# A planned sort-attention and Fourier-mix kernel: mixed V stored and gathered back with keys on partitions, in place of a mix that produces that layout directly

## Chip, core and metric

One NeuronCore of one Trainium2 chip runs the whole program. The metric is the device time of one execution in microseconds (us); less is better. Before the change three executions took 284.15, 284.58 and 284.76 us, median 284.58. The profiled execution is the one of 284.76 us; its span, from the first to the last instruction, is 283.0 us, so 1.76 us lie outside the span.

Engines: PE (matrix unit, with PEld for its weight loads), DVE (vector), ACT (scalar), POOL (GpSimd) and SP (sync). POOL and SP issue the DMAs.

## What is computed

The inputs are q, k, v of shape (4, 8, 768, 64), a sort_net of (4, 8, 8, 8) and two MLP weights, 512x2048 and 2048x512. Each of 32 (batch, head) pairs has 8 blocks of 96 tokens. The reference, cut to what matters:

```
P = sort_net
for _ in range(5):                       # Sinkhorn: rows, then columns
    P = exp(P - max(P, -1)); P = P / sum(P, -1); P = P / sum(P, -2)
k_sorted = einsum('bhij,bhjcd->bhicd', P, k_b)      # blocks of K mixed
v_sorted = einsum('bhij,bhjcd->bhicd', P, v_b)      # blocks of V mixed
attn = softmax(q_b @ k_sorted.T / 8)                # inside each block
x = attn @ v_sorted                                 # heads side by side
u = x + real(fft(fft(x, axis=tokens), axis=model))
out = u + relu(norm(u) @ w_ch1) @ w_ch2
```

## The kernel before

The four batches are worked one after another through the same stages: attention (attn), the Fourier stage in two parts (dft1, dft2), normalisation, and the MLP in two token halves (mlp(b, 0) and mlp(b, 1)). V is mixed for two batches at once: "pair 0" is batches 0 and 1, "pair 1" batches 2 and 3.

The program is written as a list of operations with costs, priorities and dependences (Plan.add). A planner (Plan.schedule) plays them through on a model of the engines when the program is built and so fixes one order for each engine and each DMA queue; on the chip every engine runs its order strictly one after another and waits by semaphores. "late" and the second number of a cost are the planner's allowances for latency; they change the order only. DMA issues are such operations too: most loads stand in POOL's order, small copies, DMA transposes and most stores in SP's. The planner drives towards a goal, the end of dft2(0, 0), since the MLP work (lines 1281 and 1302), which is most of PE's, can begin only after it. Where PE would idle before that goal, dummy matmuls ("spin", line 1397) are put into its order; their number is fixed when the program is built.

The way of V for a pair t, which the change rewrites:

- load_v (line 520) brings v with the 128 (head, block) rows of a pair on the partitions, into nat[t], as two halves of 48 tokens of each block. v_path then sums V over the 96 tokens of a block on PE with an identity weight (line 693, tag psm, 12 matmuls of 512 columns) and on DVE (line 701, tag vb), for the block means vbn.
- eight copies (pair 0, on DVE and ACT, line 678, "vcx<-hr") or eight subtractions of the mean (pair 1, on DVE, line 726) rearrange nat into vcx, in which the 96 tokens of one feature lie side by side.
- bdv_make makes the block-diagonal mixing matrix bdv16 (line 780) from the Sinkhorn result.
- v_mix (line 732) multiplies 128 columns of vcx, as weights, with bdv16: 64 matmuls of 128x128 (line 742), for pair 0 with 64 more that subtract the mean (line 745). Since vcx is the weight, the result has the tokens (keys) on the partitions. Sixteen copies of 96x512 per pair (line 678, "vsf<-bank") move it from PSUM into vsb, from which av (line 1021) reads it.

Attention of a pair of heads hp: kq matmuls (line 927) and their copies into ks, q transposes (line 957) and copies into qt, scores (line 982), exp on ACT (line 991), subtraction of one into the eb buffers (line 1004 on DVE, 1006 on ACT), av (line 1021), and on DVE the reciprocal and scaling into rt (lines 1033 and 1036). The four eb buffers are two pairs of heads. They are set to zero at the start by POOL (line 537).

From rt, DVE and PE go through dft1 (lines 1053 to 1103), y (ACT, line 1111), dft2 (lines 1181, 1185, 1169), u (lines 1193 and 1205), statistics (1219, 1221), ny (ACT, 1225 and 1228), un (1241 and 1245), transposes (1260) and ut, to the MLP.

Of the kernel before, what the change touches and what calls it, by code (L numbers as in the profile page):

```python
# [18 lines left out]
D = 64  # L19
# [25 lines left out]
GT = 384  # L45


def _consts():
# [56 lines left out]
    vrow = np.zeros((1, 128, D + 1), f16)  # L105
# [9 lines left out]
    def as32(m):  # L115
# [8 lines left out]
                rows=rows, erow=np.tile(erow, (1, 4)), vrow=vrow, pack=pack)  # L124


class Op:
    __slots__ = ("n", "costs", "fn", "preds", "succs", "left", "ready", "prio",
                 "vts", "fresh", "nbytes", "end", "start", "eng", "tag",
                 "crit", "late")  # L130
# [13 lines left out]
class Plan:  # L144
# [14 lines left out]
    def add(self, costs, fn, r=(), w=(), prio=None, nbytes=0, tag="",  # L159
            after=()):  # L160
# [7 lines left out]
        o.preds, o.succs, o.vts, o.fresh = set(after), [], [], []  # L168
        for k in r:
            o.preds.update(self.wr.get(k, ()))  # L170
# [41 lines left out]
    def schedule(self):  # L212
# [48 lines left out]
        while todo:  # L261
# [70 lines left out]
            for s in o.succs:  # L332
                s.left -= 1
                for x in s.costs:
                    s.ready[x] = max(s.ready[x],
                                     o.end + (0.03 if x == e else self.XL))
                if s.left == 0:
                    for x in s.costs:
                        avail[x].append(s)
# [13 lines left out]
def pe(t):  # L353
    return {"PE": (t, t + 0.17)}
# [12 lines left out]
def kernel(  # L367
# [22 lines left out]
    def many(name, n, shape, dtype):  # L390
# [18 lines left out]
    vcx = ct("vcx", [128, 128 * D + 2], F16)  # L409
    dtab = vcx[:, 6144:7168].rearrange("p (c w) -> p c w", c=4)  # L410
    lt = vcx[0:97, 7168:7168 + LTW]
    vsf = ct("vsf", [97, 128 * (D + 1)], F16)
    vsb = vsf[:, 0:128 * (D + 1)].rearrange("p (g w) -> p g w", w=D + 1)
    eb4 = ct("eb4", [97, 4, EW], F16)
    P.pool("eb", [eb4[:, n, :] for n in range(4)])
# [14 lines left out]
    many("un", 2, [128, DM], F16)  # L430
# [9 lines left out]
             vcx[:, 7938:8194].bitcast(F32).rearrange(  # L440
# [15 lines left out]
    phl = [hr[1].rearrange("p a b -> p (a b)")[  # L456
        0:32, 64 * n:64 * n + 64].rearrange("p (i j) -> p i j", i=NB)
        for n in range(2)]
    pk, pvh, pvl = [hr[1].rearrange("p a b -> p (a b)")[
        0:32, 1024 * n:1024 * n + 1024].rearrange("p (i x) -> p i x", i=NB)  # L460
        for n in (2, 4, 5)]
    pws = hr[1].rearrange("p a b -> p (a b)")[0:32, 3072:3232].bitcast(F32)
# [9 lines left out]
    def load(dst, src, nbytes, w, prio, eng="POOL", r=(), after=()):  # L472
# [3 lines left out]
                  prio=prio, nbytes=nbytes, tag="load", after=after)  # L476
        o.late = 6.0 if after else 0.0
# [6 lines left out]

    slot = {}
# [14 lines left out]
    def load_qk(nm, b, hf, prio):  # L500
        after = lns[1:2] if b > 1 else ()
        src = {"k": k, "q": q}[nm]
        if nm == "q" and b in QB:
            for h in range(4):
# [4 lines left out]
                    260000, [("kq", slot[nm, b, hf], h)], prio + 0.01 * h,  # L509
# [4 lines left out]
                 "h (p r) d -> p h (r d)", r=6), 786432,  # L514
# [5 lines left out]
    def load_v(t, hf, prio):  # L520
        load(nat[t].rearrange("p (c d) -> p c d", d=D)[
            :, 48 * hf:48 * hf + 48, :],
            vv[128 * t:128 * t + 128, 48 * hf:48 * hf + 48, :], 1572864,
            [("nat", t, hf)] + (hk(0)[8 * hf:8 * hf + 8] if t == 0 else
                                kqk(2 * hf) + kqk(2 * hf + 1)), prio)
# [10 lines left out]
    for n in range(4):  # L536
        P.add({"POOL": (1.5, 1.6)}, lambda _, n=n: nc.gpsimd.memset(
            eb4[0:96, n, :], 0.0), w=[("ebz", n)], prio=-4996.9, tag="ebz")
    for n in range(2):
        t_ = P.pools["ks"][n][2]  # L540
        P.add({"POOL": (0.4, 0.5)}, lambda _, t_=t_: nc.gpsimd.memset(
            t_[:, :, 96:128], 0.0), w=[("ksz", n)], prio=-4996.8, tag="ksz")
    P.add({"POOL": (0.6, 0.7)}, lambda _: nc.gpsimd.memset(
        vsb[0:96, :, D:D + 1], 1.0 / XSC), w=["vsz"], prio=-4996.8, tag="vsz")
    P.add({"POOL": (0.1, 0.4)}, lambda _: nc.gpsimd.memset(
        pmt[:, 4:7, DM:DM + 2], 0.0), w=["pmz"], prio=-4996.7, tag="small")
# [3 lines left out]
          w=["smalls"], prio=-4996.6, tag="small")  # L550
# [7 lines left out]
            "o (n s) -> o n s", n=4), 13376),  # L558
        vrow=(vsf[96:97, 0:128 * (D + 1)], cn["vrow"].ap(), 16640),
# [14 lines left out]
    load_qk("k", 0, 0, -5000.0)  # L574
    load_qk("q", 0, 0, -4999.0)
    load_v(0, 0, -4998.0)
    load_v(0, 1, -4997.0)
    load_qk("k", 0, 1, -4996.0)
    load_qk("q", 0, 1, -4995.0)
    load_c("dtab", -4994.0)  # L580
    load_c("lt", -4993.0)
    load_c("cs", 19.0)
    load_c("tab", 20.0)
    for c in range(4):
        load_w1(c, 40.0 + c)
    for hf in range(2):
        load_qk("k", 1, hf, 30.0 + hf)
        load_qk("q", 1, hf, 30.5 + hf)
    for c in range(4):
        load_w2(c, 50.0 + c)  # L590
# [4 lines left out]
    V = nc.vector  # L595

    exps = []

    def sk(c, fn):
        o = P.add(c, fn, r=["pw", "rs"] + hk(1), w=["pw", "rs"], tag="sink")  # L600
# [3 lines left out]
    for it in range(5):  # L604
# [16 lines left out]
        if it == 4:  # L621
            P.add({"DVE": (0.14, 0.21)}, lambda _: V.tensor_tensor(
                phl[0], pw, rs[:, None, :].broadcast_to([32, NB, NB]),
                op=ALU.mult), r=["pw", "rs"], w=["phi"] + hk(1), tag="pk")
# [6 lines left out]
        phl[0][:, :, :, None].broadcast_to([32, NB, NB, 16])),  # L631
        r=["phi"], w=["pk"] + hk(1), tag="pk")
    P.add({"DVE": (0.14, 0.21)}, lambda _: V.tensor_tensor(
        phl[1], pw, phl[0], op=ALU.subtract), r=["pw", "phi"],
        w=["plo"] + hk(1), tag="pk", prio=P.prio + 20)
    for n, d_ in enumerate((pvh, pvl)):
# [5 lines left out]
              r=[("phi", "plo")[n]], w=[("pvh", "pvl")[n]] + hk(1), tag="pv",  # L642
# [7 lines left out]
    P.add(pe(0.45), f, r=["pk", "pack"] + hk(1), w=[bk], tag="psk")  # L650
# [35 lines left out]
    def v_path(t):  # L686
        n3 = nat[t].rearrange("p (c d) -> p c d", d=D)
        psm = Buf("pm", "pf") if t else Buf("pm")
        stage = [i for n in range(4) for i in kqk(n)] if t else hk(0)
        for hf in range(2):  # L690
            def f(_, hf=hf):
                for n in range(6):
                    nc.tensor.matmul(
                        psm.ap, idh,
# [735 lines left out]
```

## Time and profile before

| | |
|---|---|
| median of three executions | 284.58 us |
| profiled execution | 284.76 us |
| its span | 283.0 us |
| PE busy | 269.0 us (95%) |
| DVE busy | 169.7 us (60%) |
| ACT busy | 160.7 us (57%) |
| POOL busy | 55.0 us (19%) |
| bytes moved by DMA | 26.33 MB in 42529 packets, 30106 of them under 512 B |
| first MLP matmul starts | 65.74 us |
| dummy matmuls (line 1397) | 64, 16.8 us busy |

A row of a view "by stretch" gives, for each engine, the busy time and in brackets the number of instructions, then the granted clock of PE (1.00 is full), the mean share of the 16 DMA engines (more than 1 where packets overlap) and the GB/s moved. A row of a timeline gives start, duration, engine, line, operation, tiles and count, and in brackets the idle time before it with what ended it. A row of a group gives busy time, the mean duration of one in ns, and the idle time before. Durations of neighbouring instructions overlap; what one costs when they follow one another is the distance of their starts, called a slot in the prediction.

### The profile page before, as it was taken

How to read it: one execution, taken by the hardware profiler on the slowest of the kernel's cores; microseconds unless marked ns; L12 is line 12 of the kernel's file. 1: busy time of each engine (PE TensorE's matmuls, PEld its weight loads, DVE VectorE, ACT ScalarE, POOL GpSimd, SP SyncE). 2: the span in 40 equal slices, each digit the busy share in tenths (PEclk: the TensorE clock that was granted, in tenths of full speed). 3: DMA queues.
4: the chain of work that ended last, by engine and by line, in shares of the span. 5: the costliest groups of instructions: out<-in, count | busy, mean ns of one | idle time of the engine just before them, and what ended most of it. 6: DMA issues, size and time to landing. Idle time of an engine off the chain costs nothing.

```text
span 283.0 us, 5927 instructions
## 1 busy us (share of the span) xinstructions
PE 269.0 (95%) x2356; PEld 156.7 (55%) x2356; DVE 169.7 (60%) x419; ACT 160.7 (57%) x337; POOL 55.0 (19%) x81
## 2 busy tenths in 40 slices
PE   5899999999999999999999999999999999999991
PEld 2457877555665476544566456455546545546440
DVE  4599999999999979863499414255014316310011
ACT  2589979859679767780587046327414714817200
POOL 8975313250000280001300000040000021000031
PEclk9999999999999999999999999999999999999997
DMA  7999999999101299151111020231121032111012
GB/s 110 217 254 255 212 210 210 218 189 162 39 0 31 44 186 163 31 74 49 76 43 29 36 78 0 56 113 34 38 76 39 0 87 82 37 56 39 0 74 74
DMA packets 42529, 26.33 MB, mean 93 GB/s; under 512 B 30106, under 2 KB 38824, under 8 KB 42500
## 3 DMA queue, kind: packets, MB, share of 16 engines
q0 software_dynamic: 23536, 18.31, 37.9%
q1 hardware_dynamic: 18966, 7.64, 12.8%
q8 instruction: 18, 0.29, 0.4%
q14 instruction: 9, 0.07, 0.1%
HBM read 28.96 MB, written 6.29 MB: 125 GB/s over the span
## 4 chain that ended last, share of the span: by engine, by line
issue 58%; PE 14%; DVE 13%; POOL 7%; DMA 5%; ACT 1%; POOLq 0%; DVEq 0%
DMA hr<-in_v_dram 5%; POOL out_dram L1325 4%; POOL kq L475 3%; PE bank L1281 2%; PE bank L1302 2%; PE bank L742 2%; DVE rt L1036 2%; PE bank L745 1%; DVE st L1219 1%; PE bank L1093 1%; DVE eb L1004 1%; PE bank L982 1%; DVE pmt L1053 1%; PE bank L927 1%; DVE bdk L669 1%
## 5 line engine op out<-in xcount | busy, mean ns | idle before, releaser
L1293 ACT ACTIVATE hr<-bank 128x384 f16<-128x384 f32 x110 | 54.0, 491 | 72.0 <-PE bank L1281 65.1
L1281 PE MATMUL bank<-ut,w1sb 128*128 128x384 f16 x512 | 91.5, 326 | 0.7 <-DVE vsf L678 0.4
L1302 PE MATMUL bank<-w2sb,hr 128*128 128x512 f16 x384 | 87.9, 379 | 0.0
L1281 PEld LDWEIGHTS <-w1sb 128*128 128x128 f16 x512 | 48.8, 98 | 33.9 <-issue 1.0
L1302 PEld LDWEIGHTS <-hr 128*128 128x128 f16 x384 | 36.4, 98 | 41.2
L1310 DVE TENSOR_TENSOR u<-bank,u 128x512 f32<-128x512 f32 x24 | 16.5, 689 | 67.9 <-PE bank L1302 67.8
L1325 POOL DMA_INDIRECT out_dram<-u,rows x12 | 11.7, 971 | 160.1 <-DVE u L1310 159.5
L991 ACT ACTIVATE ex<-bank 96x384 f32<-96x384 f32 x64 | 27.9, 485 | 3.1 <-PE bank L982 2.9
L1397 PE MATMUL bank<-pack 128*128 128x480 f16 x64 | 16.8, 395 | 3.3 <-DMA pack<-k_pack 3.3
L1006 ACT ACTIVATE eb<-ex,negone 96x384 f16<-96x384 f32 x32 | 19.0, 615 | 0.2
L1021 PEld LDWEIGHTS <-eb 97*128 97x128 f16 x416 | 15.8, 98 | 3.4 <-issue 1.1
L1021 PE MATMUL bank<-vsf,eb 97*128 97x65 f16 x416 | 17.1, 193 | 0.5 <-DVE un L815 0.2
L1036 DVE TENSOR_TENSOR rt<-bank,rz 128x384 f16<-128x384 f32 x32 | 17.2, 546 | 0.3
L475 POOL DMA_DIRECT2D kq<-in_q_dram x20 | 16.4, 833 | 3.1 <-DMA kq<-in_q_dram 1.2
L475 POOL DMA_DIRECT2D kq<-in_k_dram x8 | 6.4, 799 | 49.9 <-PE bank L927 48.9
L1219 DVE BATCH_NORM_STATS2 st<-u 128x6 f32<-128x512 f32 x24 | 15.9, 684 | 0.2
L1193 DVE SCALAR_TENSOR_TENSOR u<-rt,bank 128x512 f32<-128x512 f16 x12 | 8.0, 682 | 11.2 <-PE bank L1185 11.2
L1205 DVE SCALAR_TENSOR_TENSOR u<-rt,bank 128x510 f32<-128x510 f16 x12 | 7.9, 677 | 10.1 <-PE bank L1169 6.4
L678 ACT CAST vsf<-bank 96x512 f16<-96x512 f32 x17 | 12.6, 789 | 2.0 <-PE bank L742 1.9
L1241 ACT ACTIVATE un<-u,nm,ny 128x512 f16<-128x512 f32 x12 | 9.7, 810 | 6.5 <-DMA ut<-un 4.4
L678 ACT CAST ks<-bank 128x384 f16<-128x384 f32 x23 | 10.7, 478 | 3.3 <-PE bank L927 3.2
L742 PE MATMUL bank<-bdv,vcx 128*128 128x128 f16 (+1 forms) x128 | 12.0, 220 | 0.3 <-DVE vcx L726 0.3
(131 smaller groups left out, 337.1 us busy)
## 6 DMA issues: line engine op xcount, KB each, us to landing
kq<-in_k_dram POOLq DMA_DIRECT2D x8, 384.0 KB, 13.1
w1sb<-in_moe_w_ch_dram POOLq DMA_DIRECT2D x4, 512.0 KB, 16.2
w2sb<-in_moe_w_ch_dram POOLq DMA_DIRECT2D x4, 512.0 KB, 19.1
out_dram<-u SPq DMA_DIRECT2D x8, 256.0 KB, 2.1
kq<-in_q_dram POOLq DMA_DIRECT2D x4, 384.0 KB, 8.9
hr<-in_v_dram POOLq DMA_DIRECT2D x2, 768.0 KB, 13.5
kq<-in_v_dram POOLq DMA_DIRECT2D x2, 768.0 KB, 21.0
kq<-in_q_dram POOLq DMA_DIRECT2D x16, 96.0 KB, 7.1
```

The lines of the kernel that those rows point to most:

```text
L475: o = P.add({eng: c}, lambda _: e.dma_start(dst, src), r=r, w=w, prio=prio, nbytes=nbytes, tag="load", after=after)
L678: (nc.scalar.copy if e == "ACT" else V.tensor_copy)(dst, src)
L742: nc.tensor.matmul(o, vcx[:, 96 * d:96 * d + m], bd, start=True, stop=(t == 1))
L991: nc.scalar.activation(ex.ap, pss[h2].ap[0:96, 0:384], AF.Exp, scale=SCALE),
L1006: nc.scalar.activation(ed, src, AF.Identity, bias=negone[0:96])
L1021: nc.tensor.matmul(po.ap[:, 65 * T:65 * T + 65], eb.ap[:, e0:e0 + 128], vsf[:, vi:vi + 65], start=(n == 0), stop=(n == len(WIN[T]) - 1), s ...
L1036: P.add({"DVE": (0.45, 0.56)}, lambda _: V.tensor_tensor(rt.ap[:, :, D * h:D * h + D], po3()[:, :, 0:D], rz.ap[:, :, None].broadcast_to([1 ...
L1219: P.add({"DVE": (0.6, 0.69)}, lambda _, u=u, st=st: V.bn_stats(st.ap, u.ap), r=[u], w=[st], tag="bn")
L1281: nc.tensor.matmul(ps.ap[:, 0:GT], w1sb[:, c, 128 * fc:128 * fc + 128], ut.ap[:, c, :], start=(c == 0), stop=(c == 3))
L1293: nc.scalar.activation(hr[g][:, fc, :], ps.ap[:, 0:GT], AF.Relu)
L1302: nc.tensor.matmul(ps.ap, hr[g][:, fc, 128 * tt:128 * tt + 128], w2sb[:, fc, :], start=(fc == 0), stop=(fc == 15))
L1325: st_ = [nc.gpsimd.indirect_dma_start(out.rearrange("b s m -> (b s) m"), bass.IndirectOffsetOnAxis(ap=rows[:, i:i + 1], axis=0), u.ap, None)]
```

## The change

All of V's way is rewritten; the arithmetic result is the same.

- Mixing. bdv16 is now the weight and 512 columns of nat[t] stream through it: 12 matmuls of 512 columns per pair (tag vmix), for pair 0 with 12 more that subtract the mean. The result has the (head, block) rows on the partitions, and twelve copies of 128x512 per pair (tag vev) put it into hr1 (pair 0) or back into nat[1] (pair 1).
- Layout. Keys come on the partitions through DRAM: the mixed V is stored into a scratch tensor vdr in six pieces of 64 partitions x 2048 values (tag vst, 256 KB each), three for each batch, and six gathers (tag vgt) fetch it back into vsb as 32 x 64 runs of 64 values, that is 2048 runs of 128 bytes, 256 KB each. Of pair 0, the three stores of batch 0 stand in SP's order, those of batch 1 in POOL's; of pair 1 all stand in POOL's. av of a batch waits for the three gathers of its own batch only. A vsb row is padded from 65 to 80 values (VW).
- The rearranging copies into vcx are gone for pair 0. For pair 1 the mean is subtracted in place by two DVE operations of 3072 values (tag vcd), and the sums of V no longer use PE: eight DVE reductions, each over 96 tokens of 8 features (tag vb1). The two loads of V of pair 1 become six, each in 2048 runs of 256 bytes.
- Buffers. Six eb buffers in place of four (NEB); they are cleared by three DVE memsets and six ACT copies at the start in place of POOL's memsets. Three un buffers in place of two. The Sinkhorn tiles move out of hr1.
- Order of loads in POOL's queue, in full up to the MLP weights. Before: k and q of batch 0 (heads 0 to 3); v pair 0 (2); k, q (heads 4 to 7); dtab; lt; four memsets of eb; cs; tab; k, q, k, q of batch 1; w1 (4); w2 (4). After: v pair 0 (2); q, k (heads 0 to 3); k, q (heads 4 to 7); tab; k, q of batch 1 (heads 0 to 3); three gathers of batch 0; three stores of batch 1; dtab; lt; cs; k, q of batch 1 (heads 4 to 7); three gathers of batch 1; w1 (4); w2 (4). Later, before: v pair 1 (2), then k and q of batches 2 and 3. After: v pair 1 (6), k and q of batch 2, six stores and, two at a time between the indirect output stores of mlp(0, 1), six gathers of pair 1, then k and q of batch 3.
- SP's queue: the three stores of batch 0 come first; the output stores of mlp(0, 0) come ahead of the first DMA transposes of q for batch 2, where they came behind the first four of those.
- Planner's numbers (they change the order alone): longer allowances for DMA transposes, small copies, stores and loads, the new "behind" relation, and the priority of the second a_path.
- Order on PE. Up to the first MLP matmul the order has 70 dummy matmuls (64 before). From the first MLP matmul on, it holds, against before, 64 matmuls of 128x128 less (line 742), 12 of 512 columns more (vmix), 26 of av more and 8 of the scores more.

```
-        for n in range(16):
+        for n in range(12):
+            r, hf = divmod(n, 2)
             ps = Buf("pm", "pf")
...
-                    nc.tensor.matmul(o, vcx[:, 96 * d:96 * d + m], bd,
-                                     start=True, stop=(t == 1))
+                o = ps.ap.rearrange("p (c d) -> p c d", d=D)
+                nc.tensor.matmul(o, bd, n4[:, r, 8 * hf:8 * hf + 8],
+                                 start=True, stop=(t == 1))
                 if t == 0:
                     nc.tensor.matmul(
-                            o, vbn[:, d:d + 1].broadcast_to([128, m]), bd,
+                        o, bd, vbn[:, None, :].broadcast_to([128, 8, D]),
                         start=False, stop=True)
...
+            P.add({"ACT": act(512), "DVE": dve(512)},
                   lambda e, n=n, ps=ps: copy(
+                      e, vm[:, 512 * n:512 * n + 512], ps.ap),
+                  r=[ps] + vmk, w=[("vm", t, n)] + (
+                      [("nat", 1, r)] if t else []), tag="vev")
+        for hb in range(2):
+            w64 = slice(64 * hb, 64 * hb + 64)
+            for k_ in range(3):
+                cols = slice(2048 * k_, 2048 * k_ + 2048)
+                P.add({"POOL": (0.7, 7.0 if t else 4.5)} if t or hb else {"SP": (0.4, 4.2)},
+                      lambda e, w64=w64, cols=cols:
+                      (nc.gpsimd if e == "POOL" else nc.sync).dma_start(
+                          vdr[t][w64, cols], vm[w64, cols]),
...
+                o = P.add({"POOL": (1.3, 1.3)},
+                          lambda _, k_=k_, w64=w64, cols=cols:
+                          nc.gpsimd.dma_start(
+                              vsb[32 * k_:32 * k_ + 32, w64, 0:D],
+                              vdr[t][w64, cols].rearrange(
+                                  "g (c d) -> c g d", d=D)),
...
+        if t:
+            for n in range(8):
+                P.add({"DVE": (1.38, 1.48)}, lambda _, n=n: V.tensor_reduce(
+                    vb[:, 0, 8 * n:8 * n + 8],
+                    n3.rearrange("p c d -> p d c")[:, 8 * n:8 * n + 8],
+                    axis=AX.X, op=ALU.add),
...
+        for hf in range(2):
+            def f(_, hf=hf):
+                m = nat[1][:, 3072 * hf:3072 * hf + 3072].rearrange(
+                    "p (c d) -> p c d", d=D)
+                V.tensor_tensor(m, m, vbn[:, None, :].broadcast_to(
+                    [128, 48, D]), op=ALU.subtract)
...
-    for n in range(4):
-        P.add({"POOL": (1.5, 1.6)}, lambda _, n=n: nc.gpsimd.memset(
-            eb4[0:96, n, :], 0.0), w=[("ebz", n)], prio=-4996.9, tag="ebz")
+    for n in (0, 1, NEB - 1):
+        P.add({"DVE": (1.0, 1.1)}, lambda _, n=n: V.memset(
+            eb4[0:96, n, :], 0.0), w=[("ebz", n, 0), ("ebz", n, 1)],
+            prio=-190.0 if n < 2 else -20.0, tag="ebz")
+    for n in range(2, NEB - 1):
+        for hf in range(2):
+            c_ = slice(EW // 2 * hf, EW // 2 * hf + EW // 2)
+            P.add({"ACT": (0.85, 0.95)}, lambda _, n=n, c_=c_: nc.scalar.copy(
+                eb4[0:96, n, c_], eb4[0:96, 0, c_]), r=[("ebz", 0, hf)],
+                w=[("ebz", n, hf)], prio=-20.0, tag="ebz")
...
+    load_v(0, 0, -5000.0)
+    load_v(0, 1, -4999.0)
+    load_qk("q", 0, 0, -4998.0)
+    load_qk("k", 0, 0, -4997.0)
     load_qk("k", 0, 1, -4996.0)
     load_qk("q", 0, 1, -4995.0)
+    load_c("tab", -4994.5)
+    load_qk("k", 1, 0, -4994.0)
+    load_qk("q", 1, 0, -4993.0)
```

## Prediction

> **What bounds the kernel now.** I read the 40 slices first, then the sums by stretch, the chain, the timelines, the groups and the DMA view.
>
> The slices:
>
> ```profile
> PE   5899999999999999999999999999999999999991
> DVE  4599999999999979863499414255014316310011
> PEclk9999999999999999999999999999999999999997
> DMA  7999999999101299151111020231121032111012
> ```
>
> PE looks full from the second slice on, but its early work is partly dummies. DVE is full from slice 3 to 14 (14 to 99 us), the DMA engines in the first nine. The clock is granted throughout. By stretch:
>
> ```profile
> 0.00:22.00 22.00, 16.78 (x123) 8.23 (x124) 14.41 (x49) 12.12 (x17) 19.48 (x28) 1.00 1.00 201
> 22.00:55.80 33.80, 32.13 (x546) 25.15 (x547) 32.64 (x92) 31.53 (x66) 10.26 (x15) 1.00 1.18 217
> 55.80:65.70 9.90, 9.45 (x106) 5.49 (x104) 9.90 (x31) 5.62 (x14) 4.04 (x5) 1.00 1.52 192
> 65.70:277.30 211.60, 210.57 (x1589) 117.83 (x1584) 112.02 (x250) 111.44 (x242) 20.22 (x33) 1.00 0.31 57
> ```
>
> In the last row PE idles for 1.0 us of 211.6, with real work only: from the first MLP matmul on, PE is the bound. In the second row DVE works 32.6 of 33.8 us: there DVE is the bound, and PE's surplus is padding. So the time is three sums: when the first MLP matmul starts, PE's work from there, and a fixed end (283.0 - 277.3 = 5.7 us, plus 1.76 outside the span).
>
> What leads to the MLP: two pieces of the chain, and rows of three timelines.
>
> ```profile
> 3.54 13.48 DMA hr<-in_v_dram
> 17.07 1.46 PE bank L693 x6
> ```
>
> ```profile
> 9.69 0.83 ACT L678 COPY qr<-kq 128x768 f16<-128x768 f16 x1 [3.08 <-DMA kq<-in_q_dram]
> 21.98 0.28 DVE L780 TENSOR_TENSOR bdv<-bank,pack 128x128 f16<-128x128 f32 x1
> 34.55 0.20 DVE L1033 RECIPROCAL rz<-bank 128x6 f32<-128x6 f32 x1
> 55.82 1.27 DVE L1193 SCALAR_TENSOR_TENSOR u<-rt,bank 128x512 f32<-128x512 f16 x2
> 63.36 0.81 ACT L1241 ACTIVATE un<-u,nm,ny 128x512 f16<-128x512 f32 x1 [0.92 <-PE bank L1260]
> 65.74 0.50 PE L1281 MATMUL bank<-ut,w1sb 128*128 128x384 f16 x2
> ```
>
> V lands at 17.0, the mixing matrix is masked at 21.98, the first av comes back at 34.55, the first u at 55.82, the MLP starts at 65.74.
>
> **The change, part by part.**
>
> *PE's work after the MLP starts.* In slots (distance of starts): line 742 takes 0.058 us (64 of them hold 4.24 us, overlaps counted), a 512-column matmul 0.216 (six in 1.46, the last one's tail included), av 0.034, scores 0.040. Less: 64 x 0.058 = 3.7. More: 12 x 0.216 = 2.6, 26 x 0.034 = 0.9, 8 x 0.040 = 0.3. Sum +0.1 us. The 12 sums of V (2.6 us) and pair 0's mix (128 x 0.06 = 7.7 against 24 x 0.216 = 5.2) leave PE ahead of the MLP only, where PE had padding: worth nothing by themselves. So the change is worth what it does to the start of the MLP.
>
> *The front.* k lands at 7.8 (6.5 us after issue) and q at 9.7: 1.9 us each. V no longer waits for them: 17.0 - 3.8 = 13.2. Its sums take 1.46 more, 14.7. The Sinkhorn chain loses ACT's wait for q (its fifth exp, now at 12.19, could come 2.3 earlier), but three memsets stand ahead of it on DVE. None is in the trace; POOL took 6.21 us for four (1.55 each), DVE's memset of eps 0.06. I take 0.9, near the middle, as half as many 4-byte elements: Sinkhorn starts 1.1 late, and ACT's clearing copies (six at about 0.75, as a 768-element q copy) cost 0.8: fifth exp at 11.9. Then its tail, the copies for the masks, q's copy (q now lands at 15.1) and the reduction (0.65) put the first mask at 16.6, 5.4 earlier. Bounds 15.2 and 18.6 by the two memset prices.
>
> *DVE from the mask to the first u.* Before: 32.4 us of slots and 1.4 idle. The changed order holds, against it: eight vsf copies less (0.67 each, -5.3), six 512-wide copies of the mix more (+3.6; 0.60, between the 384-wide 0.47 and vsf's strided 0.67), seven line-1004 operations (-1.9) and three scalings less (-1.6), two line-654 masks and a line-669 one more (+2.3), copies of q, k and A-path rows more (+3.6), small ones +0.4. Sum +1.1: 33.5 us.
>
> ```profile
> L678 DVE CAST vsf<-bank 96x512 f16<-96x512 f32 x15 | 10.9, 779 | 0.7 <-PE bank L742 0.4 <-PE bank L745 0.3
> L726 DVE TENSOR_TENSOR vcx<-kq,vbn 128x768 f16<-128x768 f16 x8 | 11.7, 1472 | 0.0
> L701 DVE TENSOR_REDUCE vb<-bank 128x64 f32<-128x512 f32 x2 | 1.3, 673 | 0.0
> ```
>
> *The new round trip.* The mix runs from 17.1 to 22.4 on PE, its copies (six on ACT, six on DVE) end at 23.3. The third store is then issued on SP; a 32 KB copy of line 889 lands 1.9 us after its issue, 5.6 at worst in a full queue; I take 3.5: 27. The gathers are 2048 packets of 128 bytes each. The nearest packets are q's loads for batch 2, also 128 bytes:
>
> ```profile
> GB/s 158 152 146 152 152 142 162 154 158 158 156 154 211 203 160 242 197 260 232 193 193 180 205 426 172 189 164 188 209 191 203 170 184 172 170 178 188 201 213 187
> q0 software_dynamic: 1962, 0.37, 178.0%
> ```
>
> This is the stretch 62.0 to 64.5; in its first twelve fortieths, with only such packets, 155 GB/s moved: 262144 bytes in 1.7 us (bounds: 1.2 at the 210 of large loads; 1962 packets took 1.78 x 16 x 2.5 us, 36 ns each, so 4.6 if none overlapped). Queueing on POOL: issues of 256, 512 and 768 packets took 0.54, 0.75 and 0.83 us, so about 1.5 for 2048. V of batch 0 is complete at 27 + 1.5 + 1.7 + 2 = 32. Its cover is DVE's other work: 17.5 us of slots stand between mask and first reciprocal, to 34.1, 36 with idle time. Covered by 4 us; past that each us is one of the end. For scores beginning later and ACT's share I add 1.2 idle: first u at 16.6 + 33.5 + 2.6 = 52.7, against 55.82: -3.1.
>
> The Trainium skill, "DMA: Bandwidth & Descriptors", Specifications, speaks against this part: under 512 bytes a descriptor leaves line rate (read-modify-write). Its section on small descriptors gives 3 cycles of overhead on 4 beats for 128 bytes, by which a gather would take about 1.1 us (estimate, at its 425 GB/s). The row's 1.7 is used; by the page the cover grows by some 2 us and the sum stays.
>
> *POOL's queue behind the round trip.* POOL waits at the first gather for its store; behind it wait dtab, lt, cs, the last k and q of batch 1, the second gathers, w1 and w2. Loads of 786 KB of float32 take 1.9, w1 chunks 2.5. Up to q of batch 1 and the first stores 25.4; then gathers 5.1, stores 1.9, constants 2.5, k and q 3.7: that q lands at 40.5. DVE copies it in front of dft1 at about 42. Then gathers 5.1, w1 10, landing 1.9: 55.6, against need at 62. Both covered, by 1.5 and 6 us. On SP the small copies of line 889 stand behind the stores; their rows are made after 30 and read near 52: no wait. The DMA transposes of q for batch 2 now stand behind the output stores of mlp(0, 0), which PE finishes some 29 us after the MLP's start (48 matmuls of 0.216, 64 of 0.165, the rest other work), near 91; its scores stand on PE some 47 us after that start, near 109: covered by 18 less a transpose's 5.4.
>
> *From u to the MLP.* 9.9 us; the third un waited 0.92 for its buffer, now there are three: -0.4.
>
> *Pair 1.* The eight reductions are not in the trace: 0.97 by line 701 (0.65 slot for 512 elements), 1.4 by line 726, strided as they are; I take 1.4, 11.2 us; subtractions 2 x 1.85 (768 elements of f16 at 0.47). Less: eight at 1.4. So DVE gets about +3.5 between 75 and 105, where it was full; MLP work on PE (42 us for batch 0) hides it, and PE meets the mixed input at 102 only 3 to 4 us after DVE delivers. I charge 0.5 (bounds 0 and 4). The gathers of pair 1 have some 10 us before batch 2's av.
>
> The skill's "VectorE: DVE Perf Modes", perf-mode tier table, says a reduce has only the 1x mode; by that one would take 0.95 (estimate), and pair 1 would have 3.6 us more cover.
>
> *Sum.* -3.1 - 0.4 + 0.1 + 0.5 = -2.9: MLP near 62.2, profiled time 281.9. The profiled run lay 0.18 over the median: 281.7.
>
> **Rivals.**
>
> 1. *The DMA queue becomes the bound* (slower). For: nine full slices, a blocked POOL queue, twelve gathers and six V loads more in small packets. By the queue's sum above w1 lands at 45.4 + 6g for a gather of g; at g = 3.4 it reaches 65.7 and the change loses. At 4.6: 73, +7.3, 292. Against: the 155 GB/s. Chance 0.27.
> 2. *The round trip eats the front's gain.* From first reciprocal to u DVE has 15.8 us of slots and lost 0.5; u keeps 55.8 if V completes at 39: stores at 5.6 and gathers landing 7.5 after issue, as q's loads did at 62 us, give 38.5. Time 283.5 to 285.2, 284.4. For: both latencies are in the trace; against: the backlog then was larger. Chance 0.17.
> 3. *No idle at all*: mask at 15.2, 1.4 idle, page-like gathers: u at 50.1, 279. Chance 0.12.
>
> **How the numbers follow.** My forecast (279.5 to 283.5) has 0.44. A measurement here tells 0.2%, 0.57 us, from no change. Faster: 0.44 + 0.12 + 0.06 of rival 2 = 0.62; same 0.07; slower 0.04 + 0.27 = 0.31. The range 278.0 to 288.5 leaves out about 0.05 below and 0.13 above; the likeliest case's own is 279.5 to 283.5.
>
> **What would show it.** First mask near 16.6, V of batch 0 landing before 36, first u near 52.7, first MLP matmul near 62.2, and PE as full after it. A DVE or PE wait on vsf, kq or w1 loads shows rival 1 or 2; PE idle at the pair 1 mix shows that the 0.5 was too small. A first MLP matmul later than 65.7 makes the forecast wrong.

## The result and the profile after

Slower: 297.09 us, the median of four executions (295.39 to 298.33), against 284.56 us before (four executions); ratio 1.0438, 95% interval 1.0379 to 1.0497. The profiled execution is the one of 295.39 us, span 293.6 us, the fastest of the four. The ratios leave out executions that were slow against the fastest of the same kernel (by over 1.5%), so a ratio can differ from that of two medians.

The slices of the changed kernel (one digit for 7.34 us):

```profile
PE   5998987999999999913999999999999999999992
DVE  6787998899739897730696299816414415511010
PEclk9999997999999999985999999999999999999999
DMA  7998999999993508999951230211302102113002
```

PE was full from the second slice on before; now it has a hole in slices 18 and 19 (125 to 140 us), in which the granted clock falls too, and small dents in slices 4, 6 and 7. The DMA engines, quiet after 71 us before but for 99 to 113 us, are full again in slices 16 to 20 (110 to 147 us).

By stretch, with the same four cuts as before (start, first mixed work, first u, first MLP matmul):

```profile
0.00:22.00 22.00, 18.15 (x112) 8.62 (x113) 16.43 (x57) 13.85 (x23) 7.67 (x18) 1.00 1.05 191
22.00:55.90 33.90, 29.45 (x432) 19.86 (x431) 29.63 (x75) 27.26 (x63) 18.59 (x24) 0.95 1.02 211
55.90:65.20 9.30, 8.35 (x86) 4.82 (x84) 9.30 (x29) 3.48 (x8) 3.88 (x4) 1.00 1.18 210
65.20:288.10 222.90, 211.69 (x1571) 115.90 (x1566) 119.02 (x266) 106.41 (x235) 39.59 (x56) 0.98 0.56 85
```

Up to the MLP the change gained next to nothing: the MLP starts at 65.2, before at 65.7. The last row has the loss: PE works 211.7 us there, before 210.6, but the row is 222.9 us long, before 211.6. PE's idle time in it went from 1.0 to 11.2 us.

One row of PE's timeline is nearly all of it. SP's two rows and POOL's two show what was issued ahead (starts and durations of the issue, not of the transfer):

```profile
123.97 1.90 PE L1358 MATMUL bank<-w2sb,hr 128*128 128x512 f16 x8
136.65 2.72 PE L1337 MATMUL bank<-ut,w1sb 128*128 128x384 f16 x8 [10.78 <-DMA ut<-un]
```

```profile
115.81 2.52 SPq L1000 DMA_TRANSPOSE qt<-kq  x1
118.43 3.34 SPq L1308 DMA_TRANSPOSE ut<-un  x2
```

```profile
114.58 2.21 POOL L803 DMA_DIRECT2D vsf<-vdr  x2
118.91 2.17 POOL L803 DMA_DIRECT2D vsf<-vdr  x2
```

PE has finished the MLP of batch 0 at 125.87 and stands before the MLP of batch 1 until 136.65, for the DMA transposes of its normalized rows (un into ut, line 1308). The last of them was issued at 119.98, so 16.7 us before. They share the DMA engines with the gathers of pair 1: three had been issued ahead of the last transpose, and three more were issued while it was under way (120.02 to 124.28). Before the change the last transpose was on its way 2.4 us (125.90 to 128.31), and PE came to it at 134.48 without a wait (SP's and PE's timeline of before):

```profile
122.49 4.60 SPq L1252 DMA_TRANSPOSE ut<-un  x3
134.48 0.81 PE L1281 MATMUL bank<-ut,w1sb 128*128 128x384 f16 x4
```

The DMA view of 105 to 145 us of after gives the gathers (KB each, then median us from issue to landing):

```profile
vsf<-vdr POOLq DMA_DIRECT2D x6, 256.0 KB, 16.9
out_dram<-u,rows POOLq DMA_INDIRECT x3, 12.4
```

The 16.9 is a single landing, that of the fourth gather; for the other five the view has none. Run e12 below, which has the same order, has all six, with a median of 13.0.

And the clock, PE alone, in the hole and behind it (PE busy, instructions, granted clock, DMA share, GB/s):

```profile
126.00:136.00 10.00, 0.00 (x0) 0.68 1.13 185
136.00:140.00 4.00, 3.35 (x11) 0.53 1.38 121
140.00:142.00 2.00, 2.00 (x15) 1.00 1.46 115
```

After the wait PE works 3.35 us at about half its clock (0.53): about 1.6 us more.

### The profile page after: what moved, and what is told of

Its sections match the earlier page's. It is cut to its first block, busy times and chain, and to the rows that moved or that the text cites. A ratio compares the mean times of both kernels' runs of the same rounds, so it can differ in the third digit from the quotient of the medians.

```text
span 293.6 us, 5635 instructions
## 1 busy us (share of the span) xinstructions
PE 267.6 (91%) x2194; PEld 149.2 (51%) x2194; DVE 175.1 (60%) x424; ACT 151.0 (51%) x326; POOL 70.7 (24%) x102
## 4 chain that ended last, share of the span: by engine, by line
issue 48%; DMA 19%; PE 16%; DVE 8%; POOL 5%; ACT 1%; POOLq 0%; DVEq 0%
DMA kq<-in_q_dram 9%; PE bank L1358 5%; PE bank L1337 5%; DMA kq<-in_k_dram 4%; DMA out_dram<-u,rows 3%; POOL out_dram L1381 3%; DMA vsf<-vdr 2%; DMA vdr<-hr 2%; PE bank L1149 2%; DVE rt L1092 1%; DVE st L1275 1%; POOL kq L487 1%; PE bank L1237 1%; PE bank L775 1%; DVE eb L1059 1%
## 5 line engine op out<-in xcount | busy, mean ns | idle before, releaser
L1337 PE MATMUL bank<-ut,w1sb 128*128 128x384 f16 x512 | 92.1, 329 | 10.8 <-DMA ut<-un 10.8
L1061 ACT ACTIVATE eb<-ex,negone 96x384 f16<-96x384 f32 x36 | 21.3, 612 | 0.4
L1467 PE MATMUL bank<-pack 128*128 128x480 f16 x70 | 18.0, 396 | 3.3 <-DMA pack<-k_pack 3.3
L1076 PE MATMUL bank<-vsf,eb 97*128 97x65 f16 x416 | 16.9, 193 | 0.8 <-DVE rt L1092 0.2
L1076 PEld LDWEIGHTS <-eb 97*128 97x128 f16 x416 | 15.1, 98 | 3.4 <-issue 1.0
L803 POOL DMA_DIRECT2D vsf<-vdr x12 | 13.0, 1090 | 15.1 <-DMA vdr<-hr 15.1
L719 DVE TENSOR_REDUCE vb<-kq 128x8 f32<-128x768 f16 x8 | 11.4, 1465 | 2.2 <-DMA kq<-in_v_dram 2.2
L1059 DVE TENSOR_SCALAR eb<-ex 96x384 f16<-96x384 f32 x28 | 10.9, 393 | 2.7 <-ACT ex L1046 2.4
L1467 PEld LDWEIGHTS <-pack 128*128 128x128 f16 x70 | 6.8, 104 | 11.0 <-DMA pack<-k_pack 3.3
L1037 PE MATMUL bank<-qt,ks 64*128 64x96 f16 x256 | 11.9, 207 | 0.5 <-ACT ut L706 0.2
L982 PE MATMUL bank<-bdk,kq 128*64 128x128 f16 x192 | 10.0, 226 | 2.1 <-ACT ex L1046 1.1
## 6 DMA issues: line engine op xcount, KB each, us to landing
hr<-in_v_dram POOLq DMA_DIRECT2D x2, 768.0 KB, 11.1
```

Source lines behind the costliest of these rows:

```text
L1061: nc.scalar.activation(ed, src, AF.Identity, bias=negone[0:96])
L1076: nc.tensor.matmul(po.ap[:, 65 * T:65 * T + 65], eb.ap[:, e0:e0 + 128], vsf[:, vi:vi + 65], start=(n == 0), stop=(n == len(WIN[T]) - 1), s ...
L1337: nc.tensor.matmul(ps.ap[:, 0:GT], w1sb[:, c, 128 * fc:128 * fc + 128], ut.ap[:, c, :], start=(c == 0), stop=(c == 3))
L1467: nc.tensor.matmul(spin.ap[:, 0:480], idh, pack.bitcast(F16))
```

## The experiments

Theory A: the transposes for the MLP of batch 1 are held on the DMA engines by pair 1's round trip. Rival B: the loss comes from the front. Rival C: the vector engine's new work for pair 1 makes everything behind it late. "After" is the changed kernel; each time is a median of 4 to 12 executions beside the kernel before on the same chip.

| label | edit | us | ratio to before, 95% interval | PE idle ahead of or in the MLP of batch 1, us (one profiled execution each) |
|---|---|---|---|---|
| after | | 297.09 | 1.0438 [1.0379, 1.0497] | 10.8 |
| e1_ut_pe | those transposes on PE | 289.95 | 1.0174 [1.0127, 1.0220] | 0.6, then 1.3 and 0.7 |
| e2_long1 | pair 1's gathers in long runs | 288.02 | 1.0100 [1.0056, 1.0145] | 3.3 |
| e3_long01 | both pairs' gathers in long runs | 287.51 | 1.0059 [1.0021, 1.0097] | 1.5 |
| e4_late1 | pair 1's gathers planned later | 284.92 | 1.0002 [0.9973, 1.0030] | 0.5 and 0.3 |
| e5_late1_dummies | e4 and six dummies | 284.34 | 0.9994 [0.9973, 1.0015] | 1.4 |
| e6_late1_kq_first | e4, k and q ahead of the constants | 285.74 | 1.0028 [1.0002, 1.0054] | 0 |
| e7_late1_kq_early | e4, k and q ahead of the gathers | 282.60 | 0.9923 [0.9898, 0.9949] | 0 |
| e8_sum_pe | pair 1's sums on PE | 304.27 | 1.0654 [1.0613, 1.0695] | 14.4 in two waits |
| e9_late1_sum_pe | e8 and e4 | 294.51 | 1.0335 [1.0305, 1.0364] | 9.9 |
| e10_kq_early_w1 | e7, w1 behind the gathers | 280.57 | 0.9865 [0.9841, 0.9888] | 0 |
| e11_kq_early_only | e7 without e4 | 290.52 | 1.0232 [1.0198, 1.0266] | 3.0, then 0.7 |
| e12_sum_short | 12 of 96 tokens summed | 297.09 | 1.0454 [1.0415, 1.0493] | 12.2 |

### e1: the transposes taken off the DMA engines

```
-            if b > 0:
+            if b > 1:
                 P.add({"SP": (1.3, 6.0)}, lambda _, tt=tt, un=un:
                       nc.sync.dma_start_transpose(
```

> Theory A (the DMA transposes of batch 1's normalized rows share the 16 DMA engines with pair 1's six gathers, land near 135.7 us instead of some 2.4 us after issue, and PE stands idle 10.8 us before the MLP of batch 1): with those transposes made on PE (24 more 128x128 matmuls, about 1.6 us of PE), the idle of 10.8 us before the first ff1 matmul of batch 1 goes and the time falls to 285 to 289. Rival B (the loss comes from the front, before 66 us): 296 to 299, the wait is replaced by another. Rival C (the vector engine's sums and subtractions of pair 1 make the rows themselves late): 294 to 299, PE waits for the vector engine there.

289.95 us: 7.1 us come back although PE has 24 matmuls more, 1 us above the expected span. The wait of 10.78 is 0.58. Theory A stands, rival B falls for the larger part of the loss. What is left is two smaller waits (1.3 and 0.7 us near 140), which follow a wait of the vector engine for an output store (its timeline of e1), and a front of its own, with the MLP at 67.60: there the clock fell for longer than in after.

```profile
139.04 0.69 DVE L1261 SCALAR_TENSOR_TENSOR u<-rt,bank 128x510 f32<-128x510 f16 x1 [5.30 <-DMA out_dram<-u,rows]
```

### e2, e3: the same bytes in long runs

```
-                              vsb[32 * k_:32 * k_ + 32, w64, 0:D],
-                              vdr[t][w64, cols].rearrange(
-                                  "g (c d) -> c g d", d=D)),
+                              vsf[32 * k_:32 * k_ + 32,
+                                  5120 * hb:5120 * hb + 4096].rearrange(
+                                      "p (a x) -> p a x", a=2),
+                              vdr[t][w64, cols].rearrange(
+                                  "(p a) x -> p a x", a=2))
```

> Pair 1's six gathers move the same 262144 bytes each, but in long runs instead of 128-byte ones, so V of batches 2 and 3 lands in other places than the reference's; order of every engine as in the changed kernel. Theory A in its form 'small packets': the gathers end within some 2 to 3 us each, the transposes land by 124, PE's idle of 10.8 us shrinks under 2 us, time 284.5 to 288. Theory A in its form 'bytes and queueing' (any traffic of that size holds the transposes): 293 to 297. Rivals B and C: 296 to 298.

> As the run before, for both pairs: V of all batches lands in other places than the reference's; two small clearings more on POOL before the first gather. If the front's gain was eaten by the 128-byte gathers of pair 0 (q of batch 1 and w1 late behind them), the first MLP matmul moves from some 65.5 to 62 to 64 and the time is 2 to 3.5 us under that of the run before: 281.5 to 285. If the front's loss is elsewhere (the stores, the order of work), it stays within 0.7 us of the run before.

e2: 288.02, at the edge of what the form "small packets" expected. The gathers still took 8.0 us from issue to landing (the median of the two for which the view has a landing; 13.0 over all six in e12, with 128-byte runs), and PE still waited (its timeline in e2):

```profile
129.98 2.13 PE L1343 MATMUL bank<-ut,w1sb 128*128 128x384 f16 x8 [3.28 <-DMA ut<-un]
```

So, in these two executions, the 128-byte runs make up some 7.5 of the 10.8 us, and the other 3.3 stay with the same bytes in long runs, though four gathers, not three, had been issued ahead of the last transpose in e2. A count of small packets does not show the difference. The packet line is the same in after and in e2 but for the mean rate:

```profile
DMA packets 56544, 32.61 MB, mean 111 GB/s; under 512 B 42842, under 2 KB 51560, under 8 KB 56516
```

```profile
DMA packets 56544, 32.61 MB, mean 114 GB/s; under 512 B 42842, under 2 KB 51560, under 8 KB 56516
```

The gathers are not among the packets under 512 B at all: in the packet records each is 64 packets of 4096 bytes, in both kernels. The prediction's "2048 packets of 128 bytes" was thus a wrong reading. With 128-byte pieces the same packets take longer (all 4096-byte packets of POOL's queue in 102 to 140 us: mean 339 ns in after, 278 in e2).

e3: 287.51 with a wide spread (282.94 to 290.83). The profiled execution is its fastest; there the MLP starts at 63.76 against 66.02 in e2. But PE's clock fell to 0.50 near 50 us in e2's profile and not in e3's, and e12, with short runs and a clock that held, starts the MLP at 64.03. So these traces give pair 0's short runs about 0.3 us of the front, not the 2 to 3.5 expected; the spread of e3's times is too wide to settle it.

### e4: the gathers behind the transposes

```
+    for hb in range(2):
+        for o in gets[1, hb]:
+            o.preds.update(uxs)
```

Here uxs are the three transposes for mlp(1, 0).

> Pair 1's gathers are planned behind the three DMA transposes of batch 1's first group, nothing else is changed by hand (the planner moves two indirect output stores and three loads ahead of them). Theory A: the transposes land within 5 us of issue, PE's idle of 10.8 us before the MLP of batch 1 falls under 3 us; but the gathers now end near 145 to 150 and batch 2's av may wait up to 5 us for them: 285 to 292. Rivals B and C: 296 to 299, PE's idle at that place stays.

284.92 us, 12.2 less than after, and not to be told from the kernel before. Nothing is taken away; six gathers are issued from 125.35 on in place of 114.58. The MLP of batch 1 starts when PE comes to it, 6.0 us after the last transpose was issued (PE's timeline of e4):

```profile
125.71 0.38 PE L1225 MATMUL bank<-rb,vcx 97*128 97x512 f16 x1
125.93 6.01 PE L1339 MATMUL bank<-ut,w1sb 128*128 128x384 f16 x36
```

PE alone in the two stretches of e4 that answer to the hole of after:

```profile
126.00:136.00 10.00, 9.85 (x62) 1.00 1.28 187
136.00:140.00 4.00, 3.34 (x26) 1.00 1.07 137
```

In the very stretch in which after stood still PE works 9.85 of 10 us at full clock, with the DMA engines moving as much (187 GB/s, in after 185). The load is the same; what moves beside the transposes decides. The three transposes that SP issued from 115.8 on (one of q, two of un) are 1792 packets of 256 bytes: in e4 they ran from 117 to 122.4 us, in after from 118 to 134.7. The gathers land in 6.6 us here (median of the two landings in the view), and batch 2's av waits for none. From the MLP's start to PE's last matmul e4 takes 211.95 us (65.40 to 277.35), before 211.60.

### e5, e6, e7, e10: what the front lost

In e4 the MLP still starts at 65.37. The vector engine waits 2.4 us for q, 1.4 of them near 45 us; PE then waits 1.43 for the vector engine, and the clock falls (PE alone, e4):

```profile
46.00:48.00 2.00, 0.57 (x4) 0.83 1.02 145
48.00:50.00 2.00, 2.00 (x15) 0.50 1.08 158
50.00:52.00 2.00, 2.00 (x18) 0.82 1.09 221
```

e5 puts six dummies into that wait:

```
+                if o.tag == "dft1" and not seen:
+                    seen.append(o)
+                    for _ in range(6):
+                        nc.tensor.matmul(spin.ap[:, 0:480], idh,
+                                         pack.bitcast(F16))
```

> As the run with pair 1's gathers planned later (284.92 us), with six more 480-column dummy matmuls on PE just ahead of the first matmul of the Fourier stage of batch 0, where PE waited 1.43 us near 46 us. In that run PE's granted clock fell to 0.50 after that wait and was back at 1.00 some 4 us later. If the fall of the clock follows PE's wait, the clock stays at 1.00 in 46 to 52 us, the first MLP matmul comes 1 to 2 us earlier and the time is 283 to 284. If the clock falls for another reason (load of the chip, temperature), it falls again and the time stays at 284.5 to 285.5.

The same stretches of e5, PE alone:

```profile
46.00:48.00 2.00, 1.70 (x10) 1.00 1.08 145
48.00:50.00 2.00, 2.00 (x23) 1.00 1.04 174
50.00:52.00 2.00, 2.00 (x23) 1.00 1.06 215
```

The clock holds, and the MLP starts at 64.20, 1.2 us earlier. One execution does not show that the dummies did it: in e9 and e12 the clock held behind the same wait of 1.43 us (e9, PE alone), and in e7 behind one of 2.04.

```profile
46.00:48.00 2.00, 0.61 (x4) 1.00 1.03 145
48.00:50.00 2.00, 1.86 (x22) 1.00 1.08 164
```

So such a wait can let the clock fall but does not always. Over all executions the dummies made the fall rarer: the mean granted clock lies below 0.994 in six of the ten executions of e4 (0.985 to 0.999) and in one of the twelve of e5 (0.992 to 0.999). The intervals of the two ratios overlap: the gain in time is not shown.

e6 and e7 move the last k and q of batch 1 in POOL's queue, e6 ahead of the three constants, e7 ahead of the first gather:

```
-    load_qk("k", 1, 1, 31.0)
-    load_qk("q", 1, 1, 31.5)
+    load_qk("k", 1, 1, -4992.0)
+    load_qk("q", 1, 1, -4991.0)
```

This is e7; in e6 the two stand behind the gate of the first gathers, with 24.0 and 24.5.

> As the run with pair 1's gathers planned later, with the last k and q of batch 1 issued ahead of the three constant loads (about 1 MB, 4.7 us at the 210 GB/s of that stretch) instead of behind them. Theory: the 2.4 us that the vector engine waits for q, 1.4 of them near 45 us, are the front's new wait; q then lands near 41, the wait of 1.4 goes, PE's waits near 45 to 47 shrink and the clock keeps: 282 to 284. Rival: the constants are needed as soon, and the wait goes to their readers: 284.5 to 287.

> As the run with pair 1's gathers planned later, with the last k and q of batch 1 issued right after batch 0's loads, ahead of the first gather, at which POOL waits until 25.9 us. If POOL's wait in order is what makes q late, q lands near 31, the vector engine's waits for q go: 282 to 284. Rival: the 786432 bytes of each then stand ahead of the stores and gathers of V on the DMA engines, V of batch 0 lands up to 6 us later than 35 and the first reciprocal of batch 0 waits: 285 to 289.

e6 failed: q was issued 2.2 us earlier and landed at 42.7, but the planner, which counts on the landing, put q's reader further forward in its order, so the vector engine waited 3.47 us for it, PE 3.58, and the clock fell for longer (the MLP at 68.19). e7 gave 282.60, inside what was expected: q lands at 32.1, issued at 15.23, when POOL would have stood waiting for the first store until 26.5. The rival named there was real but small: the gathers of batch 0 land 2.4 to 3.1 us later than in after, and one wait moved to the gathers of batch 1, because a load of w1 had slipped ahead of them (PE's timeline of e7):

```profile
51.24 0.56 PE L1076 MATMUL bank<-vsf,eb 97*128 97x65 f16 x13 [2.04 <-DMA vsf<-vdr]
```

The MLP starts no earlier than in e4, at 65.41. What e7 gains lies behind that: 209.8 us from there to PE's last matmul, 212.0 in e4. In e7's order 26 av and 8 score matmuls stand ahead of the MLP that after and e4 have behind it, and PE idles 0.7 us less.

e10 puts w1 behind them:

```
+    gate = gets[0, 1][-1:]
     for c in range(4):
         load_w1(c, 40.0 + c)
```

> As the run with the last k and q of batch 1 loaded early and pair 1's gathers planned later (282.60 us), with the four loads of w1 issued behind the last gathers of pair 0 instead of one of them ahead. In that run PE waited 2.04 us near 49 to 51 us for those gathers, which landed at 51.1. Expected: they land 1.5 to 2.5 us earlier, that wait shrinks under 0.8, w1 lands some 2 us later and still ahead of 65: 280.8 to 282.2. Rival: w1 becomes late for the first MLP matmul, 282.6 to 284.

280.57 us, below what was expected, and 1.4% faster than the kernel before. Its stretches, with cuts at 22, at the first u (52.6) and at the MLP (62.8):

```profile
22.00:52.60 30.60, 27.84 (x431) 18.91 (x430) 27.73 (x76) 26.85 (x61) 16.23 (x21) 1.00 1.11 224
52.60:62.80 10.20, 9.64 (x122) 5.76 (x121) 10.20 (x32) 8.16 (x20) 4.64 (x4) 1.00 1.16 209
62.80:273.30 210.50, 209.86 (x1532) 114.67 (x1531) 119.14 (x259) 103.54 (x230) 39.49 (x56) 1.00 0.61 91
```

Clock 1.00 throughout, first u at 52.77, MLP at 62.80, and 0.6 us of idle behind it.

### e11: only the front mended

> The changed kernel with only the last k and q of batch 1 loaded early, pair 1's gathers as planned in the changed kernel. If the front's loss and the stall before the MLP of batch 1 add up, the gain of 2.3 us found with the later gathers shows here too: 293 to 296, with PE idle 8 to 13 us before the MLP of batch 1. If the two are one (the stall comes from the front being late), it falls to 283 to 288.

290.52: neither case. The front gained nothing here (MLP at 66.72, waits of 0.9 and 2.3 us for gathers of pair 0), and yet PE's wait before the MLP of batch 1 shrank from 10.78 to 2.97 in the profiled execution, the fastest of the four (288.74). SP's, POOL's and PE's timelines of e11:

```profile
113.92 5.35 SPq L1308 DMA_TRANSPOSE ut<-un  x2
114.56 2.14 POOL L803 DMA_DIRECT2D vsf<-vdr  x2
127.69 0.81 PE L1337 MATMUL bank<-ut,w1sb 128*128 128x384 f16 x4 [2.97 <-DMA ut<-un]
```

The gathers start when they did in after (114.58 there), but the last two transposes were issued at 113.92 and 116.62, with none and two gathers ahead of them, in place of 118.43 and 119.98 with two and three. To be ahead was not enough: the one issued at 113.92, ahead of every gather, landed at 123.2, 9.3 us after its issue, beside the last stores and the first gathers. The length of the stall is a race between two queues. Front and stall neither add up nor are they one.

### e8, e9, e12: the sums in eight parts

e8 takes pair 1's sums on PE (12 matmuls and one reduction, as pair 0 does); e9 adds e4's edit; e12 keeps the changed kernel's order and sums 12 of the 96 tokens:

```
-                    n3.rearrange("p c d -> p d c")[:, 8 * n:8 * n + 8],
+                    n3.rearrange("p c d -> p d c")[:, 8 * n:8 * n + 8, 0:12],
```

> The changed kernel with the sums of V of pair 1 taken on PE (twelve 512-column matmuls, 2.6 us, and one reduction) as for pair 0, instead of in eight reductions on the vector engine; the planner then puts all six gathers of pair 1 directly behind each other and ahead of the output stores. Theory A: the gathers still share the DMA engines with the transposes of batch 1's first group, PE stands idle there 6 to 13 us, the time is 291 to 300. Rival C (the vector engine's 11 us of sums make pair 1 late): the idle goes and the time is 284 to 288.

> The sums of V of pair 1 on PE, as two runs ago (304.27 us), and pair 1's gathers planned behind the three DMA transposes of batch 1's first group. If the eight reductions on the vector engine matter little and that run lost its time to the early gathers alone, PE's idle between 100 and 135 us goes and the time is 284.5 to 288 (2.6 us of PE more, 11 us of the vector engine less than with the later gathers alone). If the eight reductions on the vector engine are what the time needs, it stays over 292.

> The changed kernel in its own order on every engine, with each of the eight reductions of pair 1 taken over 12 of the 96 tokens, so that the block means of V of pair 1 are other numbers than the reference's. This takes some 9 to 10 us from the vector engine between 85 and 102 us. Theory A: those sums lie beside MLP work on PE, the transposes of batch 1 are still held by the gathers, PE's idle before the MLP of batch 1 stays between 8 and 13 us: 294 to 299. Rival C (the vector engine makes pair 1 late): the rows and transposes come earlier, the idle falls under 4 us: 285 to 290.

e12 answers rival C: the six reductions between 85 and 110 us fall from 8.5 to 1.6 us, and the time is 297.09, as after; PE waits 12.18 for the transposes (groups of after and of e12, PE's timeline of e12):

```profile
L719 DVE TENSOR_REDUCE vb<-kq 128x8 f32<-128x768 f16 x6 | 8.5, 1464 | 0.0
L719 DVE TENSOR_REDUCE vb<-kq 128x8 f32<-128x96 f16 x6 | 1.6, 304 | 0.0
136.92 2.72 PE L1337 MATMUL bank<-ut,w1sb 128*128 128x384 f16 x8 [12.18 <-DMA ut<-un]
```

In this order the eight reductions cost nothing that can be measured, and in e10, which has all eight, PE idles only 0.6 us behind the MLP's start. e8 was not a clean undoing, as the planner put all six gathers ahead of everything (103.9 to 111.1). The time rose over the expected span, and two other transfers became the late ones, a transpose of q and an output store, for whose buffer the vector engine waited 9.3 us ahead of its line 1276. PE's timeline of e8 (the profiled execution is the slowest of the four, 306.52):

```profile
126.50 0.50 PE L1043 MATMUL bank<-qt,ks 64*128 64x96 f16 x8 [6.20 <-DMA qt<-kq]
146.48 1.94 PE L1082 MATMUL bank<-vsf,eb 97*128 97x65 f16 x26 [8.20 <-DVE u L1276]
```

e9 stayed at 294.51, where its expectation put "the reductions are what the time needs"; e12 contradicts that reading, and the trace gives another. The planner put ten loads of k and q of batch 3 ahead, and this time an output store was held: issued at 121.72, landed at 137.14, 15.4 us (its neighbours 2.8). The vector engine waited for the buffer behind that store, and with it everything queued behind on it, the freeing of an MLP bank among it (the vector engine's and PE's timeline of e9):

```profile
137.26 0.69 DVE L1267 SCALAR_TENSOR_TENSOR u<-rt,bank 128x510 f32<-128x510 f16 x1 [15.16 <-DMA out_dram<-u,rows]
139.51 2.72 PE L1345 MATMUL bank<-ut,w1sb 128*128 128x384 f16 x8 [9.87 <-DVE u L1374]
```

In the traces of after, e8 and e9 different short transfers are late (un's transposes, a transpose of q, output stores), each beside bulk transfers issued within a few us of it. For e8 and e9 this is read from one trace each; no run took their bulk transfers away. A kernel with the sums on PE and an order otherwise equal was not tried.

## Why the prediction was wrong, step by step

The step that failed is **pair 1**: "I charge 0.5 (bounds 0 and 4). The gathers of pair 1 have some 10 us before batch 2's av." I asked only when the gathers' own reader needs them. It never waited. What I did not ask is which transfers share the DMA engines with six gathers of 256 KB: the transposes for the MLP of batch 1. The prediction follows SP's queue and POOL's each by itself and nowhere what the two move at the same time. In place of the 0.5, that stage cost 10.8 us of idle and about 1.6 of clock; e4 gives 12.2 back by order alone, and e1 gives 7.1 back by taking the transposes off the DMA engines.

The prediction also read its cover from the old order. It held that the MLP's backlog hides pair 1. Before the change the last transpose landed at 128.3 and PE came to it at 134.48, 6.2 us later. In the new order it is issued at 119.98 and PE comes to it at 125.87: with the old 2.4 us on the way, 3.5 us of cover would be left, and it took 16.7.

Of the signs that the prediction named, a first MLP matmul past 65.7 did not come (65.24), a wait on a kq load did, and PE's idle came not at the pair 1 mix but at the MLP of batch 1.

The front, step by step (predicted, then after, then e10):

| | predicted | after | e10 |
|---|---|---|---|
| first mask | 16.6 | 16.77 | 17.08 |
| V of batch 0 complete | 32 | 34.9 | 36.8 |
| first reciprocal | 36 | 36.38 | 37.75 |
| q of batch 1 (heads 4 to 7) lands | 40.5 | 44.9 | 32.1 |
| w1 complete | 55.6 | 59.6 | 58.2 |
| first u | 52.7 | 55.92 | 52.77 |
| first MLP matmul | 62.2 | 65.24 | 62.80 |

- Memsets (0.84 each, 0.9 taken), mask and first reciprocal were right. V came 2.9 us late, out of a cover of 4: no wait.
- The sum for POOL's queue was 4.4 us short for q, where the cover was 1.5. The third gather took 6.1 us from issue (28.74) to landing, and 262144 bytes in 1.7 us was a price for a free stream, not among stores, constants and small copies. This gave 1.43 us of waiting on the vector engine (the row below), then on PE, and then the half clock. In e12, with the same wait on PE and a clock that held, the MLP starts at 64.03, so the clock is about 1.2 of the 3.0 us. Rival 2 had the outcome ("the round trip eats the front's gain"), though through q, not through V.
- Rival 1 named the right kind of cause, the DMA queue as the bound on the slower side, and the wrong place: it was priced through w1, which landed 5.6 us ahead of its need. Its 292 was for a gather of 4.6 us before 66 us; the loss came at 126.
- PE's work behind the MLP's start (+0.1) was right for that order: 211.95 in e4 against 211.60. So were the reductions (1.46 each, 1.4 taken; the estimate of 0.95 from "VectorE: DVE Perf Modes", perf-mode tier table, was too low here, and no run shows why) and their being hidden (e12).
- The sum itself, 281.7, is about what the change gives once neither q nor the transposes are held up: e10 measures 280.57, with the first u and the MLP within 0.6 us of the forecast. Its way from the mask to the first u took 35.7 us, 36.1 in the sum; V came 4.8 us later than in the sum, and the first reciprocal waited 0.8. That e10 is below 281.7 is not of the sum's making: its order has the 26 av and 8 scores ahead of the MLP, and 210.5 us behind its start, where the sum has 212.2.

The vector engine's wait for q in after:

```profile
44.96 0.36 DVE L706 COPY qr<-kq 128x768 f16<-128x768 f16 x1 [1.43 <-DMA kq<-in_q_dram]
```

Added up for the profiled run: PE's last matmul was predicted at 274.4 (62.2 and 212.2) and ended at 288.1. Of the 13.7 us, 3.0 are the front and 10.7 the stage behind it.

The Trainium skill, "DMA: Bandwidth & Descriptors", Queues, rings and completion order, says that each DMA engine takes turns between the queues that have work for it, a packet at a time. The trace agrees as far as it goes: in 118 to 135 us both kinds ran, and the transposes' 256-byte packets went on until 134.7 us in after, until 122.4 in e4. That one packet waits for one of the other queue each time was not tried by itself. The DMA view of after for that stretch (queue, then packets, MB, share of 16 engines; q0 is POOL's, q1 SP's):

```profile
q0 software_dynamic: 828, 2.35, 82.9%
q1 hardware_dynamic: 1886, 0.46, 28.5%
```

The page's section on small descriptors, which I had weighed for the time of one gather, pointed the right way (e2), but no price of one gather would have shown the stall.

## What to carry to other kernels

When a change adds bulk transfers, list every short transfer that some engine needs in the same stretch, on whatever queue it is issued, and ask which will be moving at the same time; the new transfers' own reader may be the one that never waits. A cover read from the old timeline has to be read again from the new order, which may bring an engine to its next need sooner (here by 8.6 us). Try the order first: moving six issues by 11 us was worth 12.2 us here, and moving two loads and w1 another 4.3.

## What the runs showed of the hardware

- A DMA transpose of 128 KB landed 2.4 us after its issue in the kernel before. Beside 256 KB gathers issued on another queue, PE could use it only 16.7 us after its issue (after, three gathers ahead of it) and 11.1 (e11, two ahead); one with none ahead of it but gathers right behind still took 9.3 (e11). In e4, where the gathers were issued from 125.35 on and the transposes' packets had ended at 122.4, 6.0 us passed until PE came to it, and PE did not wait.
- A gather of 2048 runs of 128 bytes is recorded as 64 packets of 4096 bytes, as one in 4096-byte runs is. The count of packets under 512 B says nothing of it.
- In e4 PE's granted clock fell to 0.50 behind waits of 0.47 and 1.43 us within 2.4 us, and was back at 1.00 by 52 us. Behind waits of 0.69 and 1.43 us in e9 it stayed at 1.00. The skill's "TensorE: Matmul & The Clock Gate", What's actually happening, puts the fall after an idle window of about 3.4 us. Here less idle time was enough in some executions and not in others.
